# Routing constants in a pool of their own, and a second expert layer with tokens as the stationary side

## The chip, the cores and the metric

The program runs on one core of a Trainium2 chip. The metric is device time in microseconds, lower is better: the median of three runs of the whole program, weights and activations read from the chip's main memory and the result written back to it. Per core there are TensorE (PE, with its weight loads shown apart as PEld), VectorE (DVE), ScalarE (ACT), GpSimd (POOL) and SyncE (SP), which issues most of the transfers.

## The reference

Sliding-window attention over 2304 tokens (4 x 576, 8 heads of 64), then a dense layer pair 512 -> 2048 -> 512 with ELU, then eight experts with 288 tokens each, chosen by a greedy assignment over all sorted logits. Cut to the last part, which the change touches most:

```python
cap = N // E                                   # 2304 // 8 = 288
order = np.argsort(-(x @ w_gate).flatten())
for idx in order:
    tok, e = (int(idx) // E, int(idx) % E)
    if assigned[tok] >= 0 or counts[e] >= cap:
        continue
    assigned[tok] = e
    counts[e] += 1
for e in range(E):
    mask = assigned == e
    h = np.maximum(x[mask] @ w1[e], 0.0)       # (288, 512) @ (512, 1024)
    out[mask] = h @ w2[e]                      # (288, 1024) @ (1024, 512)
```

## The kernel before

**Stages.** Attention goes in 18 chunks of 128 tokens. The first dense layer (`layer1`, L374) goes in six token tiles (256, 256, 256, 512, 512, 512), the second (`layer2`, L470) in 18 chunks; these are woven with attention for as long as it lasts. `gate(t)` (L422) computes the logits of a tile from the hidden values with a precomputed product (L429, L430). Then `routing` (L574) finds the assignment in seven phases on VectorE and POOL, while TensorE works through layer two of the last three tiles (L482) in an order fixed by a table. Last comes the expert stage, one expert after the other.

**Precision.** From the second tile on each factor is a pair of fp16 parts, high and low, and each product is three matmuls: high x high, high x low, low x high.

**First layer of tiles 4 and 5.** For each f, twelve matmuls (L404) fill a PSUM bank `ps_mm` (three of them), ACT reads it into a buffer r (three of them; L407, L408), POOL and DVE make the ELU of it (L413, L414), POOL writes the high half g (L418), DVE the low half (L419). The r buffer is free after L419.

**Routing constants.** `routing_consts(rpool)` (L510) makes some twenty constants on POOL (L520 to L559) in the pool `rpool`, which also holds routing's working tiles. `rpool` and `slabB` (the g of tile 4) are opened when attention's pool is closed, and take its memory.

**The expert stage.** Assigned tokens stand in 24 groups of G = 96, three for each expert. Rows are gathered by an indirect DMA on POOL (L828), transposed (by TensorE for expert 0, L840; by DMA transposes otherwise, L849), and multiplied with W1 (L883: 96 matmuls of 288 columns), with ReLU on ACT (L888) and the low half on DVE (L889). The second layer keeps a 128 x 128 piece of W2 as the stationary side and streams the 288 tokens: 4 output blocks x 8 f x 3 products = 96 matmuls (L917), for the last expert in three thirds of 96 columns, 288 matmuls. Its result is transposed against the order of rows: ACT writes it to OT (L922), TensorE transposes it back in four fp32 transposes per group (L870), ACT evicts again (L872), and POOL scatters the rows (L858).

**The order.** Tile, the scheduler, sorts instructions by priority and a simulated timeline. `weave` interleaves generators by the cost that they yield. In the expert stage ACT and DVE keep program order (`dv`).

Of the kernel before, what the change touches and what calls it, by code (L numbers as in the profile page):

```python
# [7 lines left out]
F32 = mybir.dt.float32  # L8
# [31 lines left out]
def attention_moe_moe2_kernel(ctx: ExitStack, tc: tile.TileContext, q, k, v, w_in, w_out, w_gate, w1, w2, out):  # L40
    nc = tc.nc
# [8 lines left out]
    G = 96  # L50
# [459 lines left out]
    def routing_consts(pool):  # L510
        r = rt
        r["p"] = pool
# [310 lines left out]

    def gather(e):
        for j in range(3):
            XE[e, j] = moe.tile([G, 2 * DM], F16, name="xe", bufs=4)
            a = 3 * e + j
            g = nc.gpsimd.indirect_dma_start(out=XE[e, j], out_offset=None, in_=x2d[:, :],  # L828
                                             in_offset=bass.IndirectOffsetOnAxis(ap=idx[:, a:a + 1], axis=0))
        if e == 0:  # L830
            last["gather"] = g.ins


    def xe_first():
        XET[0] = moe.tile([128, 2, ND, CAP], F16, name="xet")
        for j in range(3):
            px = bank("tp", 2, [128, 2, ND, G], F16)
            for a in range(2):
                for d in range(ND):
                    nc.tensor.transpose(px[:, a, d], XE[0, j][:, (a * ND + d) * 128:(a * ND + d + 1) * 128],  # L840
                                        ident16[:G, :G])
            (nc.scalar.activation(XET[0][:, :, :, j * G:(j + 1) * G], px, AF.Copy) if j % 2 else
             nc.vector.tensor_copy(XET[0][:, :, :, j * G:(j + 1) * G], px))
            yield 400

    def xe_t(e):
        XET[e] = moe.tile([128, 2, ND, CAP], F16, name="xet")
        for j in range(3):
            nc.sync.dma_start_transpose(out=XET[e].rearrange("p a d c -> p (a d) c")[:, :, j * G:(j + 1) * G], in_=XE[e, j])  # L849
            yield 400  # L850
# [4 lines left out]
    def scatter(e, j, orow):  # L855
        a = 3 * e + j
        nc.gpsimd.memset(spacer, 0.0)
        st = nc.gpsimd.indirect_dma_start(out=out, out_offset=bass.IndirectOffsetOnAxis(ap=idx[:, a:a + 1], axis=0),  # L858
                                          in_=orow, in_offset=None)
        for o in scat:  # L860
            tc.declare_no_dep(st.ins, o.ins, reason="other rows")
        scat.append(st)


    def o_rows(e):
        yield 450
        for j in range(3):
            po = bank("pv", 1, [128, ND, 128])
            for d in range(ND):
                nc.tensor.transpose(po[:G, d], OT[e][:, d, j * G:(j + 1) * G], ident)  # L870
            orow = moe.tile([G, DM], F32, name="orow")
            dv(nc.scalar.activation(orow, po[:G], AF.Copy))  # L872
            scatter(e, j, orow)
            yield 450

    def expert(e, xe=None, tail=None):
# [20 lines left out]
        for j in range(3 if first else 0):  # L897
            next(xe, None)
            for f in range(first):
                products(phs[f], f, slice(j * G, j * G + G))  # L900
# [8 lines left out]
        OT[e] = moe.tile([128, ND, CAP], F32, name="oT")  # L909

        for r in [slice(j * G, j * G + G) for j in range(3)] if e == E - 1 else [slice(0, CAP)]:
            n = r.stop - r.start

            def add(po, d, f, m):
                w = W2[e][f // 2]
                for a, b in ((0, 0), (0, 1), (1, 0)):
                    nc.tensor.matmul(po[:, :n], w[:, a, f % 2, d * 128:(d + 1) * 128], H2[e][:, b, f, r],  # L917
                                     start=m == 0, stop=m == 3 * NF2 - 1)
                    m += 1

            def leave(po, d):
                dv(nc.scalar.activation(OT[e][:, d, r], po[:, :n], AF.Copy, scale=2.0 ** -18))  # L922

            if r.start == 0:

                pos = [bank(("sc", "tp")[d % 2], 2) for d in range(ND)]
                for f in range(NF2):
                    for d in range(ND):
                        add(pos[d], d, f, 3 * f)
                    yield 1475 * n / CAP  # L930
                for d in range(ND):
                    leave(pos[d], d)
                continue
            for d in range(ND):
                po = bank(("sc", "tp")[d % 2], 2)
                for f in range(NF2):
                    add(po, d, f, 3 * f)
                leave(po, d)
                yield 2950 * n / CAP
                if tail is not None and d == 0:  # L940
                    next(tail)
# [23 lines left out]
    w64_ctx.close()  # L965
    a2.append(a2_ctx.enter_context(tc.tile_pool(name="a2", bufs=2)))
# [9 lines left out]
    routing_consts(rpool)  # L976
# [37 lines left out]
    for e in range(E):  # L1014
        if e == E - 1:
            tail = o_rows(e)
            next(tail)
        ss = [(expert(e, xe_first() if e == 0 else None, tail if e == E - 1 else None), 24000.0)]
# [4 lines left out]
        if e > 0:  # L1023
            ss.append((o_rows(e - 1), 2000.0))
        weave(*ss)
    weave((tail, 1))
# [30 lines left out]
```

## Time and profile before

| | us |
|---|---|
| median of 3 runs | 792.12 (789.75 to 794.94) |
| profiled execution | 792.14 |
| its span, first to last instruction | 790.1 |
| TensorE busy | 742.5 (94%), mean granted clock 0.97 |
| VectorE busy | 427.7 (54%) |
| ScalarE busy | 374.0 (47%) |
| POOL busy | 184.2 (23%) |

Busy times are unions over the span, and matmuls are pipelined: the step from one matmul's start to the next one's start tells the cost of one in a dense stream, and the duration shown for one matmul is longer than that. The granted clock is 1.00 at 2.4 GHz and 0.50 at 1.2 GHz. The expert stage is the last fourth of the span.

### The profile page before, as it was taken

The numbers are of one execution on the slowest core, as the hardware profiler recorded it, in microseconds if no ns is written. First come the engines' busy times: TensorE is split into PE (matmuls) and PEld (weight loads), VectorE is DVE, ScalarE is ACT, GpSimd is POOL, SyncE is SP. The second block draws the span as 40 slices with busy tenths as digits, with TensorE's granted clock in tenths as the row PEclk, the third lists the DMA queues.
The fourth block names the chain that finished last, engine by engine and source line by source line (L and its number), as shares of the span: only waits on it lengthen the run. The fifth ranks groups of instructions, "written<-read, shape, count | busy, mean of one in ns | idle before, by whom it ended". The sixth has DMA issues, their size and how long they took to land.

```text
span 790.1 us, 16243 instructions
## 1 busy us (share of the span) xinstructions
PE 742.5 (94%) x6610; PEld 479.6 (61%) x6610; DVE 427.7 (54%) x1001; ACT 374.0 (47%) x903; POOL 184.2 (23%) x290
## 2 busy tenths in 40 slices
PE   6886988899999999889999999999989999999996
PEld 4665867655555555534545444444468888888886
DVE  3799499823332665455453555555726555555530
ACT  4467797655634654344455221010025565555632
POOL 3000000000001435344461433434141221211102
PEclk9898999999999999979999999999979999999999
DMA  9995357436455542001000211220058788987401
GB/s 279 319 216 134 62 131 194 114 82 143 96 116 113 94 67 81 3 0 54 2 24 31 81 53 41 73 75 28 15 134 266 193 252 245 261 248 201 170 22 51
DMA packets 137658, 94.06 MB, mean 119 GB/s; under 512 B 116592, under 2 KB 116592, under 8 KB 137584
## 3 DMA queue, kind: packets, MB, share of 16 engines
q1 hardware_dynamic: 134512, 83.59, 39.8%
q0 software_dynamic: 3072, 9.44, 4.6%
q8 instruction: 52, 0.85, 0.5%
q14 instruction: 22, 0.18, 0.1%
HBM read 73.68 MB, written 9.44 MB: 105 GB/s over the span
## 4 chain that ended last, share of the span: by engine, by line
PE 75%; DVE 10%; DMA 5%; ACT 4%; issue 2%; POOL 2%; SPq 1%; POOLq 0%; DVEq 0%
PE ps_mm L482 23%; PE ps_mm L404 17%; PE ps_mm L883 12%; PE ps_sc L917 6%; PE ps_tp L917 6%; DMA slab<-in_moe_w_in_dram 2%; PE ps_pv L312 2%; PE ps_tp L302 2%; DMA wg<-in_moe_w_gate_dram 1%; PE ps_pv L870 1%; PE ps_sc L651 1%; DVE b L106 1%; ACT slab L111 1%; ACT sm L290 1%; DVE r L414 1%
## 5 line engine op out<-in xcount | busy, mean ns | idle before, releaser
L482 PE MATMUL ps_mm<-slab,g 128*128 128x512 f16 x864 | 211.8, 381 | 0.0
L404 PE MATMUL ps_mm<-xt,slab 128*128 128x512 f16 (+1 forms) x960 | 177.8, 343 | 7.8 <-DVE r L414 6.9
L404 PEld LDWEIGHTS <-slab 128*128 128x128 f16 x960 | 93.0, 99 | 79.3 <-issue 12.8
L482 PEld LDWEIGHTS <-g 128*128 128x128 f16 x864 | 74.4, 98 | 71.4 <-issue 2.2
L883 PE MATMUL ps_mm<-xet,slab 128*128 128x288 f16 (+1 forms) x840 | 102.7, 281 | 0.0
L883 PEld LDWEIGHTS <-slab 128*128 128x128 f16 x840 | 78.4, 101 | 17.5
L917 PEld LDWEIGHTS <-slab 128*128 128x128 f16 x960 | 78.6, 98 | 16.2
L818 DVE SCALAR_TENSOR_TENSOR slab<-raw,slab 128x512 f16<-128x512 f32 x112 | 72.9, 688 | 20.3 <-ACT slab L817 17.8
L462 POOL TENSOR_TENSOR xs<-r,xs 128x512 f16<-128x512 f32 x17 | 20.0, 1178 | 261.3 <-ACT xs L494 230.6
L407 ACT ACTIVATE r<-ps_mm 128x512 f32<-128x512 f32 x64 | 38.6, 602 | 72.3 <-PE ps_mm L404 58.6
L917 PE MATMUL ps_sc<-h,slab 128*128 128x288 f16 (+1 forms) x480 | 70.2, 262 | 0.0
L917 PE MATMUL ps_tp<-h,slab 128*128 128x288 f16 (+1 forms) x480 | 69.9, 262 | 0.0
L414 DVE TENSOR_TENSOR r<-ps_mm,r 128x512 f32<-128x512 f32 x64 | 44.0, 688 | 38.6 <-POOL r L413 29.2
L817 ACT ACTIVATE slab<-raw 128x512 f16<-128x512 f32 x112 | 64.5, 620 | 0.0
L889 DVE SCALAR_TENSOR_TENSOR h<-ps_mm,h 128x288 f16<-128x288 f32 x64 | 29.2, 456 | 63.6 <-ACT h L888 58.1
L419 DVE TENSOR_TENSOR g<-r,g 128x512 f16<-128x512 f32 x64 | 45.9, 722 | 32.2 <-POOL g L418 26.4
L493 ACT ACTIVATE r<-ps_mm 128x512 f32<-128x512 f32 x17 | 10.2, 599 | 108.4 <-PE ps_mm L482 108.4
L290 ACT ACTIVATE sm<-ps_sc,mx 128x128 f32<-128x128 f32 x144 | 50.8, 380 | 19.4 <-DVE mx L288 19.0
L888 ACT ACTIVATE h<-ps_mm 128x288 f16<-128x288 f32 x64 | 26.3, 411 | 48.1 <-PE ps_mm L883 47.2
L858 POOL DMA_INDIRECT out_dram<-orow,idx x24 | 22.2, 926 | 114.5 <-ACT orow L872 113.1
L413 POOL TENSOR_SCALAR r<-r 128x512 f32<-128x512 f32 x48 | 38.5, 802 | 41.0 <-ACT r L408 39.9
L408 ACT ACTIVATE r<-r 128x512 f32<-128x512 f32 x64 | 40.7, 638 | 1.5
(209 smaller groups left out, 1047.2 us busy)
## 6 DMA issues: line engine op xcount, KB each, us to landing
raw<-in_moe_w_dram SPq DMA_DIRECT2D x32, 1024.0 KB, 5.4
slab<-in_moe_w_in_dram SPq DMA_DIRECT2D x16, 512.0 KB, 9.7
st<-in_moe_w_out_dram SPq DMA_DIRECT2D x16, 512.0 KB, 5.5
x2d<-xs SPq DMA_DIRECT2D x18, 256.0 KB, 2.0
vp<-in_v_dram SPq DMA_DIRECT2D x34, 128.0 KB, 3.8
qn<-in_q_dram SPq DMA_DIRECT2D x16, 256.0 KB, 3.8
kn<-in_k_dram SPq DMA_DIRECT2D x16, 256.0 KB, 5.0
vn<-in_v_dram SPq DMA_DIRECT2D x16, 256.0 KB, 3.4
```

The lines of the kernel that those rows point to most:

```text
L290: nc.scalar.activation(P[c, blk][:, i], SC[blk][:, i], AF.Exp, bias=mx[:, blk, i:i + 1], accum_out=rs[:, blk, i:i + 1])
L404: nc.tensor.matmul(ph[:, i], wi[d, (f + i) // 8][:, a, (f + i) % 8 * 128:((f + i) % 8 + 1) * 128], XT[t][:, b, d, :n], start=m == 0, stop= ...
L407: nc.scalar.activation(r, ph, AF.Relu, scale=-1.0 / A_H)
L408: last["act"] = nc.scalar.activation(r, r, AF.Exp, scale=-1.0).ins
L413: nc.gpsimd.tensor_scalar(r, r, -1.0, A_H, op0=OP.add, op1=OP.mult)
L414: nc.vector.tensor_tensor(r, ph, r, op=OP.max)
L419: nc.vector.tensor_tensor(lo, r, hi, op=OP.subtract)
L482: pe(nc.tensor.matmul(px, g[:, f % fg, a, 128 * i:128 * i + 128], wo[f // 2][:, b, f % 2, :], start=m == 0, stop=m == 3 * NF - 1))
L817: dv(nc.scalar.activation(t[:, 0, c], st[:, g], AF.Copy, scale=64.0))
L818: dv(nc.vector.scalar_tensor_tensor(t[:, 1, c], st[:, g], 64.0, t[:, 0, c], op0=OP.mult, op1=OP.subtract))
L883: nc.tensor.matmul(ph[:, r], W1[e][d][:, a, f * 128:(f + 1) * 128], XET[e][:, b, d, r], start=m == 0, stop=m == 3 * ND - 1)
L917: nc.tensor.matmul(po[:, :n], w[:, a, f % 2, d * 128:(d + 1) * 128], H2[e][:, b, f, r], start=m == 0, stop=m == 3 * NF2 - 1)
```

## The change

Group size G becomes 128, so that the 2304 assigned tokens stand in 18 chunks. An expert's 288 tokens are 2.25 chunks: `share(c)` tells which experts have rows in chunk c. Twelve chunks belong to one expert, six to two. Gathers and scatters go by chunk (18 of each instead of 24), and what is transposed goes by the parts that a chunk and an expert have in common (`parts_of`), cut where a DMA transpose needs it.

The second expert layer is turned round: the tokens' hidden values H2 are the stationary side and W2 streams with 512 columns, so PSUM holds rows, which ACT evicts once and POOL scatters. OT and the transposes L870 are gone. In a chunk shared by two experts, the stationary side is cut into 64 or 32 tokens, each written to its own partitions of one PSUM bank: chunks 4 and 13 in halves, chunks 2, 6, 11 and 15 in quarters.

The routing constants get a pool `rconsts` of their own and are made ahead of layer two's first chunk.

```diff
-    G = 96
+    G = 128
@@ routing_consts
-        r["p"] = pool
@@ the expert stage
+    def share(c):
+        out = []
+        for e in range(E):
+            lo, hi = max(G * c, CAP * e), min(G * c + G, CAP * e + CAP)
+            if lo < hi:
+                out.append((e, lo - CAP * e, hi - CAP * e, lo - G * c))
+        return out
+
+    def chunks_of(e):
+        return [c for c in range(NG) if any(x[0] == e for x in share(c))]
...
     def gather(e):
...
+        for c in chunks_of(e):
+            if c in XE:
+                continue
+            XE[c] = moe.tile([G, 2 * DM], F16, name="xe", bufs=5)
+            nc.gpsimd.indirect_dma_start(out=XE[c], out_offset=None, in_=x2d[:, :],
+                                         in_offset=bass.IndirectOffsetOnAxis(ap=idx[:, c:c + 1], axis=0))
+
+    def parts_of(e):
+        return [(c, s0, s1, p0) for c in chunks_of(e) for x, s0, s1, p0 in share(c) if x == e]
...
     def xe_first():
...
+        for c, s0, s1, p0 in parts_of(0):
+            n = s1 - s0
...
     def xe_t(e):
...
+        for c, s0, s1, p0 in parts_of(e):
+            while s0 < s1:
+                n = min(s1 - s0, 128 if p0 == 0 else 64 if p0 == 64 else 32)
+                nc.sync.dma_start_transpose(out=XET[e].rearrange("p a d c -> p (a d) c")[:, :, s0:s0 + n],
+                                            in_=XE[c][p0:p0 + n])
+                s0, p0 = s0 + n, p0 + n
             yield 400
...
-    def o_rows(e):
-        yield 450
-        for j in range(3):
-            po = bank("pv", 1, [128, ND, 128])
-            for d in range(ND):
-                nc.tensor.transpose(po[:G, d], OT[e][:, d, j * G:(j + 1) * G], ident)
-            orow = moe.tile([G, DM], F32, name="orow")
-            dv(nc.scalar.activation(orow, po[:G], AF.Copy))
-            scatter(e, j, orow)
-            yield 450
+    def o_rows(c):
+        held = share(c)
+        step = G if len(held) == 1 else 64 if all(x[3] % 64 == 0 for x in held) else 32
+        po = bank(("sc", "tp")[c % 2], 2)
+        m = 0
+        for f in range(NF2):
+            for a, b in ((0, 0), (0, 1), (1, 0)):
+                for e, s0, s1, p0 in held:
+                    for k in range(0, s1 - s0, step):
+                        nc.tensor.matmul(po[p0 + k:p0 + k + step], H2[e][:, a, f, s0 + k:s0 + k + step],
+                                         W2[e][f // 2][:, b, f % 2, :], start=m == 0, stop=m == 3 * NF2 - 1)
+                m += 1
+            yield 650
+        orow = moe.tile([G, DM], F32, name="orow")
+        dv(nc.scalar.activation(orow, po, AF.Copy, scale=2.0 ** -18))
+        scatter(c, orow)
@@ expert
-        for j in range(3 if first else 0):
+        for c, s0, s1, p0 in parts_of(e) if first else ():
             next(xe, None)
             for f in range(first):
-                products(phs[f], f, slice(j * G, j * G + G))
+                products(phs[f], f, slice(s0, s1))
...
+        for c in chunks_of(e):
+            if share(c)[-1][0] == e:
+                yield from o_rows(c)
@@ the main program
     w64_ctx.close()
+    routing_consts(ctx.enter_context(tc.tile_pool(name="rconsts", bufs=1, side="right")))
     a2.append(a2_ctx.enter_context(tc.tile_pool(name="a2", bufs=2)))
...
     rpool = late.enter_context(tc.tile_pool(name="rpool", bufs=2))
-    routing_consts(rpool)
+    rt["p"] = rpool
```

**Where instructions stand.** First POOL, where tile 4's first layer begins (r and g are its hidden values, k the first constants). Before:

```order
L413 TENSOR_SCALAR r<-r 128x512 x3
L520 IOTA k_3859 128x96
L520 IOTA k_3862 128x96
L520 IOTA k_3864 128x96
L530 MEMSET wt 32x128 x4
...
L559 MEMSET done 128x144
L418 TENSOR_SCALAR g<-r 128x512 x3
L534 AFFINE_SELECT third<-third 96x96
```

After:

```order
L413 TENSOR_SCALAR r<-r 128x512 x3
L418 TENSOR_SCALAR g<-r 128x512 x3
L413 TENSOR_SCALAR r<-r 128x512
L418 TENSOR_SCALAR g<-r 128x512
L413 TENSOR_SCALAR r<-r 128x512 x2
```

The constants now stand ahead of POOL's first L462 of layer two, and nothing is left between the L413 and the L418.

Second DVE at the same place, from attention's last L330 on (L432 reads out a chunk of gate(3) from one of two PSUM banks). Before:

```order
L330 SCALAR_TENSOR_TENSOR xt<-ps_pv,xt 128x4x128
L432 TENSOR_REDUCE logits<-ps_tp 128x8 x4
L419 TENSOR_TENSOR g<-r,g 128x512 x3
L414 TENSOR_TENSOR r<-ps_mm,r 128x512 x2
L419 TENSOR_TENSOR g<-r,g 128x512
```

After:

```order
L330 SCALAR_TENSOR_TENSOR xt<-ps_pv,xt 128x4x128
L419 TENSOR_TENSOR g<-r,g 128x512
L432 TENSOR_REDUCE logits<-ps_tp 128x8
L419 TENSOR_TENSOR g<-r,g 128x512
L432 TENSOR_REDUCE logits<-ps_tp 128x8
L419 TENSOR_TENSOR g<-r,g 128x512
L432 TENSOR_REDUCE logits<-ps_tp 128x8 x2
L414 TENSOR_TENSOR r<-ps_mm,r 128x512
```

The L419 have moved ahead of the reductions, and on ACT L408 has moved up behind the first L407.

Third PE in expert 1, where chunk 2 (32 rows of expert 0, h_6904, and 96 of expert 1, h_7243) is computed. Two of its matmuls stand between first-layer matmuls (L903, which is L883 before):

```order
L903 MATMUL ps_mm<-xet,slab 128x288
L888 LDWEIGHTS h_7243
L888 MATMUL ps_sc<-slab,h_7243 32x512
L888 LDWEIGHTS h_6904
L888 MATMUL ps_sc<-slab,h_6904 32x512
L903 LDWEIGHTS slab
L903 MATMUL ps_mm<-xet,slab 128x288
```

Most of the chunk follows the expert's first layer in one piece, three quarters of one expert and one of the other in turn:

```order
L888 LDWEIGHTS h_6904
L888 MATMUL ps_sc<-slab,h_6904 32x512
L888 LDWEIGHTS h_7243
L888 MATMUL ps_sc<-slab,h_7243 32x512
L888 LDWEIGHTS h_7243
L888 MATMUL ps_sc<-slab,h_7243 32x512
L888 LDWEIGHTS h_7243
L888 MATMUL ps_sc<-slab,h_7243 32x512
```

Before, W2's full 128 x 128 pieces (L917) and the transposes (L870) stood at these places.

## Rows read from the trace of the kernel before

**Rows 1.** The page's first part: engine, busy us, share of the span, instructions.
```profile
PE 742.5 (94%) x6610; PEld 479.6 (61%) x6610; DVE 427.7 (54%) x1001; ACT 374.0 (47%) x903; POOL 184.2 (23%) x290
```

**Rows 2.** By stretches: length, busy of PE, PEld, DVE, ACT, POOL; clock, DMA, GB/s.
```profile
332.10:339.08 6.98, 0.99 (x12) 0.66 (x13) 4.40 (x5) 3.19 (x6) 4.22 (x16) 0.60 0.01 2
339.08:343.70 4.62, 4.62 (x11) 1.57 (x11) 3.33 (x5) 0.04 (x1) 3.68 (x5) 0.50 0.00 0
...
600.00:782.60 182.60, 182.60 (x1691) 150.62 (x1688) 91.23 (x159) 100.45 (x220) 34.34 (x37) 1.00 0.70 197
```

**Rows 3.** Timeline of POOL: start, us, instruction, idle before and its releaser.
```profile
177.38 1.16 POOL L462 TENSOR_TENSOR xs<-r,xs 128x512 f16<-128x512 f32 x1 [168.87 <-ACT xs L494]
...
328.88 1.83 POOL L520 IOTA k<- 128x96 f32 x3 [12.17 <-PE ps_pv L312]
...
332.61 0.21 POOL L559 MEMSET done<- 128x144 bf16 x1
332.80 1.77 POOL L418 TENSOR_SCALAR g<-r 128x512 f16<-128x512 f32 x3
...
335.02 0.28 POOL L547 TENSOR_SCALAR_AFFINE_SELECT tri<-tri 128x128 bf16<-128x128 bf16 x1
```

**Rows 4.** Timelines of VectorE, ScalarE and TensorE in the same pause.
```profile
333.44 3.61 DVE L419 TENSOR_TENSOR g<-r,g 128x512 f16<-128x512 f32 x3 [1.24 <-POOL g L418]
...
335.88 1.20 ACT L407 ACTIVATE r<-ps_mm 128x512 f32<-128x512 f32 x2 [6.50 <-DVE g L419]
...
339.08 5.02 PE L404 MATMUL ps_mm<-xt,slab 128*128 128x512 f16 x12 [1.76 <-DVE r L414]
```

**Rows 5.** TensorE's timeline in the expert stage, and one group by line and form.
```profile
603.78 0.53 PE L917 MATMUL ps_sc<-h,slab 128*128 128x288 f16 x3
...
607.08 0.53 PE L917 MATMUL ps_tp<-h,slab 128*128 128x288 f16 x3
...
624.49 0.60 PE L870 MATMUL ps_pv<-ident,oT 128*96 128x128 f32 x4
624.93 0.53 PE L917 MATMUL ps_sc<-h,slab 128*128 128x288 f16 x3
...
781.62 1.18 PE L917 MATMUL ps_tp<-h,slab 128*128 128x96 f16 x24
...
L917 PE MATMUL ps_sc<-h,slab 128*128 128x96 f16 x144 | 9.0, 206 | 0.0
```

**Rows 6.** TensorE's timeline around small tiles, and durations of two lines.
```profile
178.03 0.81 PE L482 MATMUL ps_mm<-slab,g 128*128 128x512 f16 x3
178.77 0.69 PE L312 MATMUL ps_pv<-pt,vn 128*64 128x64 f32 x16
179.39 0.66 PE L248 MATMUL ps_tp<-ident,kn 128*128 128x128 f32 x4
179.97 0.41 PE L263 MATMUL ps_sc<-masks,identb 64*64 64x512 bf16 x4
180.32 0.39 PE L482 MATMUL ps_mm<-slab,g 128*128 128x512 f16 x1
...
L312 PE MATMUL ps_pv<-pt,vn x304: 218/222/369, 16.8 to 328.5; 128*64 128x64 f32 x144, 64*64 64x64 f32 x8
...
557.38 0.23 PE L659 MATMUL ps_sc<-co,third 96*32 96x8 f16 x3
...
L659 PE MATMUL ps_sc<-co,third 96*32 96x8 f16 x105 | 8.1, 171 | 0.0
```

**Rows 7.** Timelines of VectorE, POOL and TensorE between routing and the experts.
```profile
549.84 0.93 POOL L733 TENSOR_SCALAR i<-i 128x864 f16<-128x864 f16 x1
...
570.19 2.02 DVE L773 TENSOR_TENSOR oB<-sa,i 128x864 f16<-128x864 f16 x2
...
575.84 1.17 POOL L828 DMA_INDIRECT xe<-x2d,idx  x1 [12.22 <-DMA x2d<-xs]
...
579.36 0.80 PE L840 MATMUL ps_tp<-ident,xe 96*128 96x96 f16 x8 [3.14 <-DMA xe<-x2d,idx]
```

More of the change, by code (lines that the diff above doesn't have):

```diff
@@ L822, in split_expert @@
                 yield 500
-    def gather(e):
-        for j in range(3):
[L826 to L831, printed above, removed]
+    def share(c):
[7 more added lines that the diff above has]
+        return [c for c in range(NG) if any(x[0] == e for x in share(c))]
+    def gather(e):
+        for c in chunks_of(e):
[6 more added lines that the diff above has]
+        return [(c, s0, s1, p0) for c in chunks_of(e) for x, s0, s1, p0 in share(c) if x == e]
     def xe_first():
         XET[0] = moe.tile([128, 2, ND, CAP], F16, name="xet")
-        for j in range(3):
+        for c, s0, s1, p0 in parts_of(0):
+            n = s1 - s0
             px = bank("tp", 2, [128, 2, ND, G], F16)
@@ L839, in xe_first @@
                 for d in range(ND):
[L840 to L843, printed above, removed]
+                    nc.tensor.transpose(px[:, a, d, :n], XE[c][p0:p0 + n, (a * ND + d) * 128:(a * ND + d + 1) * 128],
+                                        ident16[p0:p0 + n, p0:p0 + n])
+            (nc.scalar.activation(XET[0][:, :, :, s0:s1], px[:, :, :, :n], AF.Copy) if c % 2 else
+             nc.vector.tensor_copy(XET[0][:, :, :, s0:s1], px[:, :, :, :n]))
             yield 400
@@ L847, in xe_t @@
         XET[e] = moe.tile([128, 2, ND, CAP], F16, name="xet")
-        for j in range(3):
-            nc.sync.dma_start_transpose(out=XET[e].rearrange("p a d c -> p (a d) c")[:, :, j * G:(j + 1) * G], in_=XE[e, j])
+        for c, s0, s1, p0 in parts_of(e):
[4 more added lines that the diff above has]
+                s0, p0 = s0 + n, p0 + n
             yield 400
@@ L853, in attention_moe_moe2_kernel, with scatter @@
     spacer = consts.tile([1, 1], F32)
-    def scatter(e, j, orow):
-        a = 3 * e + j
+    def scatter(c, orow):
         nc.gpsimd.memset(spacer, 0.0)
-        st = nc.gpsimd.indirect_dma_start(out=out, out_offset=bass.IndirectOffsetOnAxis(ap=idx[:, a:a + 1], axis=0),
+        st = nc.gpsimd.indirect_dma_start(out=out, out_offset=bass.IndirectOffsetOnAxis(ap=idx[:, c:c + 1], axis=0),
                                           in_=orow, in_offset=None)
@@ L862, in scatter, with expert @@
         scat.append(st)
-    def o_rows(e):
-        yield 450
-        for j in range(3):
-            po = bank("pv", 1, [128, ND, 128])
-            for d in range(ND):
-                nc.tensor.transpose(po[:G, d], OT[e][:, d, j * G:(j + 1) * G], ident)
-            orow = moe.tile([G, DM], F32, name="orow")
-            dv(nc.scalar.activation(orow, po[:G], AF.Copy))
-            scatter(e, j, orow)
-            yield 450
-    def expert(e, xe=None, tail=None):
+    def o_rows(c):
[14 more added lines that the diff above has]
+        scatter(c, orow)
+    def expert(e, xe=None):
         H2[e] = moe.tile([128, 2, NF2, CAP], F16, name="h2")
@@ L908, in expert @@
             yield 1475
[L909 to L941, printed above, removed]
+        for c in chunks_of(e):
+            if share(c)[-1][0] == e:
+                yield from o_rows(c)
     UT = 256 * 192 / 2.4
@@ L1014, in attention_moe_moe2_kernel @@
     for e in range(E):
[L1015 to L1018, printed above, removed]
+        ss = [(expert(e, xe_first() if e == 0 else None), 24000.0)]
         if e + 1 < E:
@@ L1022, in attention_moe_moe2_kernel @@
         ss.append((chain(take(sp, 8 if e < E - 1 else 0), xe_t(e + 1) if e < E - 1 else iter(()), sp), 9400.0))
-        if e > 0:
-            ss.append((o_rows(e - 1), 2000.0))
         weave(*ss)
-    weave((tail, 1))
 _INS = ['q', 'k', 'v', 'moe_w_in', 'moe_w_out', 'moe2_w_gate', 'moe2_w1', 'moe2_w2']
```

## The prediction

> **What bounds the kernel now.** I read the page's busy times first: TensorE is busy for 94% of the span [rows 1], so only idle time of TensorE, slow time of its clock, or matmul work itself is worth anything. The table by stretches then shows where it is not dense. From 600 to 782.6 us, the expert stage, it is busy for 182.60 of 182.60 us at full clock: there the time is the sum of the matmuls. From 332.1 to 339.08, between the gate of tile 3 and the first layer of tile 4, it works 0.99 us out of 6.98, and from 339.08 to 343.7 it is busy all the time at clock 0.50, which is 1.2 GHz [rows 2]. The change touches both places. Its two halves are independent, so I cost them apart.
>
> **A, the constants.** POOL's timeline shows the cause of the pause. The constants stand in POOL's queue ahead of three L418, the high halves of tile 4's first hidden values. The first constant waits 12.17 us for the attention's last L312, since rpool takes attention's memory. Then the constants run from 328.88 to 332.82, and only then come the three L418, with five more constants behind them until 335.30 [rows 3]. VectorE's three L419 need those L418. They begin at 333.44 and last 3.61 us together; the first is over only shortly before ACT starts again at 335.88, half a microsecond after POOL's last constant, so it made little headway beside POOL's work. ACT was waiting for the r buffer which that L419 frees, and PE's L404 follows 3.2 us behind ACT [rows 4]. TensorE queues L404 behind the second gate's first matmuls, which wait for the same L419.
>
> After the change the constants run ahead of layer two. POOL's first work there waits 168.87 us before it begins at 177.38 [rows 3], so some 4.7 us of constants are hidden; if that cover were gone, they would cost at most those 4.7. The first L418 still waits for the attention's memory, until 328.88. Three L418 then end at 330.65. By the measured half microsecond the first L419 ends at 331.2, ACT resumes at 331.25 instead of 335.88 (4.6 us earlier), and since the new order puts L408 directly behind the first L407, one 0.6 us step leaves the chain. Some of that is lost where VectorE now has L419 ahead of the reductions that free the gate's PSUM banks: I take 0.2 off. L404 resumes near 334.1: 5.0 us gained. The clock: eleven L404 ran at 1.2 GHz in 4.62 us [rows 2], so half of that, 2.3 us, was lost to the clock. It fell inside the old pause; the new one is some 2 us with gate matmuls in it, and nothing shows whether it still falls. I take 1.0 of 2.3. A = 6.0 us, with 5.0 and 7.3 as its ends.
>
> **B, the second expert layer.** Before: 672 matmuls of 288 columns. The rows at 603.78 and 607.08 have 27 between them, 0.122 us each: 82.1 us. Expert 7 has 288 of 96 columns. 24 of these take 1.18 us; without the last one's own 0.21 that is 0.042 for each of 23 steps: 12.1 us. 24 groups of four transposes at 0.44 us (from the group's start to the next matmul's) make 10.6 us [rows 5]. Together 104.8.
>
> After: 12 chunks lie inside one expert, each of 24 matmuls of 512 columns. A step of that size is 0.21 to 0.22 us (three L482 in 0.81 us, the last one's 0.39 taken off) [rows 6]; I use 0.216: 62.2 us. Six chunks straddle two experts. Two of these are cut into halves of 64 rows, four into quarters of 32, and each part streams all 512 columns: 480 matmuls. The sum rests on whether the two or four parts run beside each other. No row shows four quarters. Two neighbours do: L263's four 64x64 tiles of 512 columns take 0.41 us together, where one matmul alone has 0.39, and L482 starts only 0.35 after them; L312's 16 instructions on 64-column halves take 0.69 us, of which the last one's own duration is 0.22, so 0.47 us from the first start to the last [rows 6]. Four fp32 transposes of 128 columns take 0.44 [rows 5], so 64 such columns stream for 0.055; fifteen steps in series would be 0.83, not 0.47. Halves run side by side, so I take quarters to do so too, at 0.216 us a round.
>
> From the instruction order I count rounds. The scheduler puts small pieces of a shared chunk between first-layer matmuls; a round that is cut costs as much as a full one. The six chunks need 26, 24, 26, 26, 24 and 25 rounds, 151 in all, 32.6 us. They stand in 29 pieces, and each piece changes the shape of the array twice. Entering costs 0.09 us (L482's third start is 178.46, L312 begins at 178.77, 0.31 instead of 0.216) and leaving 0.10 (last L312 start 179.24, 0.055 of streaming, next start 179.39) [rows 6]: 29 x 0.19 = 5.5 us. After: 62.2 + 32.6 + 5.5 = 100.3. B = 4.5, less 0.2 for staggered starts: 4.3 us. ScalarE also drops its OT evictions, but in this stage it is no limit, so that counts nothing; the loads, splits and gathers are as many bytes as before and TensorE waited for none of them in 182.6 us. The last scatter has 128 rows instead of 96 behind one eviction less: nil, within 0.5 either way.
>
> By the Trainium skill ("TensorE: Matmul & The Clock Gate", Part 3, The mechanism), a weight load overlaps running matmuls only when its row group differs, and column parts all share their rows. By that rule each round would wait for its loads and the result is the third rival's. The rows of L312 speak against it: two loads and two matmuls fit in each 0.06 us (0.47 over 8 pairs) [rows 6], hardly more than the streaming alone.
>
> **C, what it costs.** Larger groups make the last two routing comparisons L773 (2.02 us) a third longer, 0.67, of which I take 0.5 since L766 and L768 shrink by a quarter. VectorE's part of x2d's last rows stands behind them, and the gather waits for that write until 575.84. POOL's L733 (0.93 us) grows by 0.3 beside VectorE's routing chain. The first gather carries 128 rows, and PE's first transpose at 579.36 waits for it [rows 7]: 0.4. Expert 0's first transposes and products come in parts of 128, 128 and 32 at the low clock: 0.6. C = 1.8, between 0.8 and 3.
>
> **Sum.** 6.0 + 4.3 - 1.8 = 8.5 us off the profiled execution's 792.14 (span 790.1 and 2 around it), which is the median, 792.12. Predicted: 783.6, own range 780 to 787.
>
> **The rivals.** First, the pause at 332 stays: the release of attention's memory still holds the L418, and if VectorE or PE's order holds L404 to nearly its old time, A falls to 1 and the time is 788.6. For it: the L418 wait for the same release. Against: four of the seven microseconds are plainly constants. Second, C is larger, the gathers above all, at twice the cost or more: 786 to 788. Third, the quarters' weight loads stand in front of their streams. Three L659 of 32 columns, load and matmul, take 0.23 us, the last one's own 0.17 among them, so a step of 0.03 [rows 6]. Four steps per round are 0.12, and 151 rounds make 18 us: 801.7, slower than before. It decides from 0.056 us a round (8.5 over 151). Fourth, parts do not run together at all: 480 x 0.216 = 103.7 instead of 32.6, 71 us more, 854.5; the L312 rows all but exclude it.
>
> **How the numbers follow.** Main case 0.70; pause stays 0.10; larger C 0.09; loads in front 0.08; no overlap 0.03. One per cent, about what a measurement here can tell, is 784.2 below and 800.0 above. Of the main case about two thirds lie below 784.2, which with its upside gives faster 0.46; same 0.43, from the rest of it and the next two; slower 0.11 from the last two. The range 779.5 to 790.5 holds the main case and most of the next two.
>
> **What the profile would show.** A right: L418 starting within 0.2 us of attention's last L312, L404 back by 334.5. B right: 32-row matmuls starting four at a time every 0.216 us, no L870, the stage from expert 0's first product to the end some 4 us shorter. Wrong if rounds are 0.27 us or longer, if TensorE idles between experts, or if L404 comes back after 337.

## The result, and the profile after

The change makes the kernel faster: 782.86 us median of 11 runs (781.48 to 788.34) against 792.56 for the kernel before in the same comparison, a ratio of 0.989 with a 95% interval of 0.987 to 0.991. The prediction was 783.6, in a range of 779.5 to 790.5. The profiled execution took 781.48 us (span 779.6), against 792.14 (span 790.1).

The first part of the page after, with the same columns as [rows 1]:

```profile
PE 736.7 (94%) x6322; PEld 430.1 (55%) x6322; DVE 427.0 (55%) x1001; ACT 358.9 (46%) x857; POOL 176.2 (23%) x272
```

TensorE has 5.8 us less to do and waits some 4.7 us less. POOL's timeline shows where the constants went, and that the three L418 now come right behind attention, beside [rows 3]:

```profile
155.88 1.83 POOL L519 IOTA k<- 128x96 f32 x3 [148.27 <-DVE slab L112]
...
160.27 0.28 POOL L546 TENSOR_SCALAR_AFFINE_SELECT tri<-tri 128x128 bf16<-128x128 bf16 x1
178.12 1.16 POOL L462 TENSOR_TENSOR xs<-r,xs 128x512 f16<-128x512 f32 x1 [17.57 <-ACT xs L494]
...
329.64 2.28 POOL L418 TENSOR_SCALAR g<-r 128x512 f16<-128x512 f32 x3 [12.19 <-PE ps_pv L312]
```

The constants run from 155.9 to 160.6, and POOL still has 17.57 us to spare before its first L462. VectorE, ScalarE and TensorE behind the L418, beside [rows 4]:

```profile
330.77 0.68 DVE L419 TENSOR_TENSOR g<-r,g 128x512 f16<-128x512 f32 x1
...
331.48 0.60 ACT L407 ACTIVATE r<-ps_mm 128x512 f32<-128x512 f32 x1 [1.36 <-DVE g L419]
...
334.46 4.60 PE L404 MATMUL ps_mm<-xt,slab 128*128 128x512 f16 x12 [0.29 <-DVE r L414]
```

L404 is back at 334.46 instead of 339.08, although this execution was 0.75 us later at attention's end (the last group of L312 began at 328.80, before at 328.05). What is left of the pause, and of the low clock behind it, beside [rows 2]:

```profile
331.40:334.46 3.06, 2.45 (x77) 2.26 (x76) 2.60 (x8) 2.95 (x6) 1.32 (x2) 0.50 0.03 8
334.46:338.23 3.77, 3.77 (x9) 1.28 (x9) 2.54 (x4) 0.35 (x1) 3.39 (x5) 0.50 0.00 0
```

TensorE idles for 0.6 us of these 6.8, but the clock is at 0.50 throughout; before, the low stretch lasted until 343.7.

For the expert stage I take the stretch from the end of expert 0's first three groups of products to TensorE's last matmul, in which both kernels have the same first-layer work. Before and after:

```profile
588.34:783.46 195.12, 195.11 (x1792) 160.33 (x1788) 100.64 (x176) 108.70 (x238) 36.12 (x39) 1.00 0.69 195
```

```profile
582.00:773.37 191.37, 191.37 (x1504) 112.78 (x1500) 101.06 (x176) 93.43 (x192) 28.87 (x28) 1.00 0.66 198
```

Both are busy from end to end at full clock, so the difference, 3.75 us, is the difference of the two second layers. In after, TensorE's timeline of chunk 2 shows the quarters. The scheduler cuts a chunk into pieces between first-layer matmuls (L903), and not always at a full round, hence counts that are no multiples of four; two earlier pieces, of 1 and 7 quarters, complete the 96:

```profile
606.77 0.40 PE L888 MATMUL ps_sc<-slab,h 128*32 128x512 f16 x3
607.10 3.12 PE L903 MATMUL ps_mm<-xet,slab 128*128 128x288 f16 x24
610.14 0.39 PE L888 MATMUL ps_sc<-slab,h 128*32 128x512 f16 x2
610.47 1.65 PE L903 MATMUL ps_mm<-xet,slab 128*128 128x288 f16 x12
612.04 0.39 PE L888 MATMUL ps_sc<-slab,h 128*32 128x512 f16 x2
612.37 1.64 PE L903 MATMUL ps_mm<-xet,slab 128*128 128x288 f16 x12
613.94 4.71 PE L888 MATMUL ps_sc<-slab,h 128*32 128x512 f16 x81
618.58 1.68 PE L888 MATMUL ps_tp<-slab,h 128*128 128x512 f16 x7
```

From 613.94 to 618.58 there are 21 rounds in 4.64 us, 0.216 each with 0.10 for the way out: a round of four quarters costs what one whole matmul does. One cut round stands from 612.04 to 612.37, 0.33 instead of 0.216; and from 610.47 to 612.04 twelve L903 take 1.57, of which 12 x 0.1225 (the step from one start to the next) = 1.47 are their own. So a piece costs 0.10 us on the way in and 0.11 on the way out.

Between routing and the experts, beside [rows 7]:

```profile
543.50 1.17 POOL L732 TENSOR_SCALAR i<-i 128x1152 f16<-128x1152 f16 x1
...
563.99 2.62 DVE L772 TENSOR_TENSOR oB<-sa,i 128x1152 f16<-128x1152 f16 x2
...
570.23 1.19 POOL L839 DMA_INDIRECT xe<-x2d,idx  x1 [12.70 <-DMA x2d<-xs]
...
573.85 1.01 PE L852 MATMUL ps_tp<-ident,xe 128*128 128x128 f16 x8 [3.33 <-DMA xe<-x2d,idx]
```

L732 and L772 are longer by the third that their tiles grew (0.24 and 0.60 us); from the gather's issue to the first transpose it is 3.62 us, against 3.52 before.

### The profile page after: what moved, and what is told of

It is laid out like the page before. It is cut to its first block, busy times and chain, and to the rows that moved or that the text cites. A ratio compares the mean times of both kernels' runs of the same rounds, so it can differ in the third digit from the quotient of the medians.

```text
span 779.6 us, 15588 instructions
## 1 busy us (share of the span) xinstructions
PE 736.7 (94%) x6322; PEld 430.1 (55%) x6322; DVE 427.0 (55%) x1001; ACT 358.9 (46%) x857; POOL 176.2 (23%) x272
## 4 chain that ended last, share of the span: by engine, by line
PE 65%; issue 14%; DVE 11%; ACT 5%; DMA 3%; POOL 2%; SPq 1%; POOLq 0%; DVEq 0%
PE ps_mm L482 23%; PE ps_mm L404 17%; PE ps_mm L903 6%; PE ps_sc L888 3%; PE ps_tp L888 2%; PE ps_pv L312 2%; PE ps_tp L302 2%; PE ps_mm L392 2%; ACT sm L290 1%; POOL out_dram L873 1%; PE ps_sc L650 1%; DVE b L106 1%; ACT slab L111 1%; DVE r L414 1%; DVE slab L106 1%
## 5 line engine op out<-in xcount | busy, mean ns | idle before, releaser
L404 PE MATMUL ps_mm<-xt,slab 128*128 128x512 f16 (+1 forms) x960 | 178.0, 343 | 6.1 <-DVE r L414 5.2
L404 PEld LDWEIGHTS <-slab 128*128 128x128 f16 x960 | 93.3, 100 | 77.7 <-issue 10.9
L903 PE MATMUL ps_mm<-xet,slab 128*128 128x288 f16 (+2 forms) x840 | 101.6, 277 | 0.0
L903 PEld LDWEIGHTS <-slab 128*128 128x128 f16 x840 | 75.2, 98 | 25.2 <-issue 6.0
L888 PEld LDWEIGHTS <-h 128*32 128x32 f16 (+2 forms) x768 | 43.1, 98 | 53.0 <-issue 9.8
L407 ACT ACTIVATE r<-ps_mm 128x512 f32<-128x512 f32 x64 | 38.5, 602 | 66.5 <-PE ps_mm L404 59.1
L414 DVE TENSOR_TENSOR r<-ps_mm,r 128x512 f32<-128x512 f32 x64 | 44.0, 688 | 36.3 <-POOL r L413 26.8
L419 DVE TENSOR_TENSOR g<-r,g 128x512 f16<-128x512 f32 x64 | 44.6, 700 | 31.8 <-POOL g L418 25.9
L888 PE MATMUL ps_sc<-slab,h 128*32 128x512 f16 (+2 forms) x384 | 53.4, 381 | 0.0
L888 PE MATMUL ps_tp<-slab,h 128*32 128x512 f16 (+2 forms) x384 | 53.0, 380 | 0.0
L413 POOL TENSOR_SCALAR r<-r 128x512 f32<-128x512 f32 x48 | 38.5, 802 | 38.5 <-ACT r L408 37.7
L462 POOL TENSOR_TENSOR xs<-r,xs 128x512 f16<-128x512 f32 x17 | 20.0, 1177 | 110.0 <-ACT xs L494 79.3
L418 POOL TENSOR_SCALAR g<-r 128x512 f16<-128x512 f32 x48 | 31.4, 655 | 47.0 <-DVE r L414 28.2
L408 ACT ACTIVATE r<-r 128x512 f32<-128x512 f32 x64 | 40.7, 638 | 1.5
## 6 DMA issues: line engine op xcount, KB each, us to landing
slab<-in_moe_w_in_dram SPq DMA_DIRECT2D x16, 512.0 KB, 10.5
```

The costliest lines, as they stand in the source:

```text
L404: nc.tensor.matmul(ph[:, i], wi[d, (f + i) // 8][:, a, (f + i) % 8 * 128:((f + i) % 8 + 1) * 128], XT[t][:, b, d, :n], start=m == 0, stop= ...
L407: nc.scalar.activation(r, ph, AF.Relu, scale=-1.0 / A_H)
L408: last["act"] = nc.scalar.activation(r, r, AF.Exp, scale=-1.0).ins
L413: nc.gpsimd.tensor_scalar(r, r, -1.0, A_H, op0=OP.add, op1=OP.mult)
L414: nc.vector.tensor_tensor(r, ph, r, op=OP.max)
L419: nc.vector.tensor_tensor(lo, r, hi, op=OP.subtract)
```

## The experiments

The theory: the two halves of the change are independent. A, the constants' place in POOL's queue, gives 5 to 6 us; B, the turned second layer, gives some 4, since a round of parts costs as much as one whole matmul and only the changes of shape cost extra; C, the larger groups, takes 2 back. C has no run of its own; it is read from the traces. The rivals are those of the prediction, and one more: that chance in TensorE's clock, which differs from execution to execution, made the difference. All runs of one comparison share the runs of the kernel before (medians 791.4 to 792.6).

**Each half alone.** a_alone has only the constants' new place:

```diff
 in before:
-        r["p"] = pool
...
     w64_ctx.close()
+    routing_consts(ctx.enter_context(tc.tile_pool(name="rconsts", bufs=1, side="right")))
...
-    routing_consts(rpool)
+    rt["p"] = rpool
```

> The kernel before with one edit: the constants go to a pool of their own and are made ahead of layer two; group size and second expert layer stay. Theory (the constants in POOL's queue were the pause): L404 is back within 6 us of attention's last L312 instead of 11, the last L482 ends some 6 us earlier than before, the expert stage is as long as before: 786.5 us (785.0 to 788.5). Rival 1 (the release of attention's memory or VectorE's order holds L404 and the changed kernel got its gain from elsewhere): 790 or more. Rival 2 (the gain is chance in the clock at the start of the program): 792.

Measured: 786.88 us, ratio 0.9927 (0.9901 to 0.9952). b_alone is the changed kernel with that one edit undone:

```diff
 in after:
-    routing_consts(ctx.enter_context(tc.tile_pool(name="rconsts", bufs=1, side="right")))
...
     rt["p"] = rpool
+    routing_consts(rpool)
```

> The changed kernel with one edit undone: the constants stand in rpool again, behind attention; G = 128 and the turned second layer stay. Theory (the two halves are independent): what is left of 9.7 us after 6.1 for the constants, so 3.6 faster than before: 789.0 us (787.0 to 790.5), with the pause of 7 us at 332 as before. Rival (the expert stage alone brings nearly all of it): 785 or less. Rival (the larger groups cost what the second layer gives): 792 or more.

Measured: 789.16 us, ratio 0.9964 (0.9943 to 0.9986). TensorE's L404 behind the pause and the expert stage (from expert 0's first products, as above) in a_alone:

```profile
333.33 4.56 PE L404 MATMUL ps_mm<-xt,slab 128*128 128x512 f16 x12 [0.30 <-DVE r L414]
```

```profile
579.65:774.78 195.13, 195.12 (x1792) 160.35 (x1789) 100.30 (x176) 108.34 (x238) 38.15 (x40) 1.00 0.69 197
```

and in b_alone:

```profile
341.05 2.29 PE L404 MATMUL ps_mm<-xt,slab 128*128 128x512 f16 x5 [1.70 <-DVE r L414]
```

```profile
589.69:781.07 191.38, 191.38 (x1504) 112.82 (x1500) 101.13 (x176) 93.61 (x192) 29.30 (x28) 1.00 0.65 198
```

The expert stage repeats to 0.01 us: 195.12 and 195.13 with the old second layer, 191.37 and 191.38 with the new one. L404 comes back 5.20 us after the start of attention's last matmul in a_alone and in after, 9.68 in b_alone and 10.56 before. By the medians A is 5.3 us and B less C is 3.0, together 8.4 (8.6 by the ratios), inside the interval of the whole (7.4 to 10.3 us). The halves add up, and no rival of the two expectations holds.

**The constants a little later.** Two things could have made the old pause: that the L418 stood behind the constants, and that POOL's work beside it held up VectorE's L419 (the first of the three in [rows 4] took 2.41 us by itself, the line below the edit). consts_late keeps the constants behind attention but calls for them after tile 5's first layer, so that the scheduler puts them behind the three L418:

```diff
 in before:
-        r["p"] = pool
...
-    routing_consts(rpool)
+    rt["p"] = rpool
...
+    routing_consts(rpool)
     pinned.append(1)
```

The first L419 of the pause in the kernel before:

```profile
333.44 2.41 DVE L419 TENSOR_TENSOR g<-r,g 128x512 f16<-128x512 f32 x1 [1.24 <-POOL g L418]
```

> The kernel before with the constants moved only a little: still behind attention in rpool, but in POOL's queue after the first three L418 instead of ahead of them. Theory (two things made the pause: the place in POOL's queue, and VectorE's L419 being slow beside POOL's constants): L418 starts at attention's end as in a_alone, but the first L419 takes some 2 us instead of 0.68 and L413 stands behind the constants, so L404 is back some 2 to 3 us earlier than before: 789.5 us (788 to 791). Rival (the place in the queue alone): as a_alone, 786.9. Rival (POOL's work beside VectorE alone, or the constants' length wherever they stand): 792.

Measured: 790.08 us, ratio 0.9978 (0.9962 to 0.9994). POOL, VectorE and TensorE in consts_late:

```profile
328.74 2.28 POOL L418 TENSOR_SCALAR g<-r 128x512 f16<-128x512 f32 x3 [12.19 <-PE ps_pv L312]
330.99 1.82 POOL L519 IOTA k<- 128x96 f32 x3
...
334.99 0.62 POOL L413 TENSOR_SCALAR r<-r 128x512 f32<-128x512 f32 x1
```

```profile
329.87 0.68 DVE L419 TENSOR_TENSOR g<-r,g 128x512 f16<-128x512 f32 x1
...
331.57 0.67 DVE L419 TENSOR_TENSOR g<-r,g 128x512 f16<-128x512 f32 x1
...
335.64 0.69 DVE L414 TENSOR_TENSOR r<-ps_mm,r 128x512 f32<-128x512 f32 x1 [2.79 <-POOL r L413]
...
338.58 2.70 DVE L419 TENSOR_TENSOR g<-r,g 128x512 f16<-128x512 f32 x3
```

```profile
336.39 5.95 PE L404 MATMUL ps_mm<-xt,slab 128*128 128x512 f16 x18 [3.19 <-DVE r L414]
```

The time is as the theory said, the way there only in part. The first three L419 are not slowed: 0.68 beside L418, 1.01 for the next, and 0.67 beside the first constants (L519), as in a_alone, without constants there (0.68, 1.01, 0.68). The loss against a_alone is the queue: L413, the next step of the ELU, waits behind the constants until 334.99 (331.69 in a_alone), L414 behind L413, and L404 comes back 8.03 us after attention's last matmul began, 2.8 later than in a_alone. So a constant costs the time for which the next needed POOL instruction stands behind it, and moving it behind one such instruction only hands the wait to the next. L419 can still be slow beside POOL: the next three here take 2.70 us, from 338.58 on, beside three L418 (from 337.93). And the last five constants have no L419 beside them here; in b_alone they do, as in the kernel before, and two of them take 0.71 and 0.62 us (0.27 and 0.20 here). So this run does not clear those five. Why the first L419 took as much as 2.41 us in the kernel before is not settled: in b_alone, with the same POOL instructions in the same order, the three of them took 2.77 us instead of 3.61.

**What holds the rest of the pause.** After the change the L418 still wait 12.19 us for attention's memory. g_free gives tile 4's first two g buffers from slabA, where two are free at that point:

```diff
 in after:
-    l4, l5 = layer1(4, [slabB] * 8), layer1(5, [slabB] * 2 + [slabA] * 6)
+    l4, l5 = layer1(4, [slabA] * 2 + [slabB] * 6), layer1(5, [slabB] * 4 + [slabA] * 4)
```

> The changed kernel with tile 4's first two g buffers from slabA, where two are free, instead of slabB, which waits for attention's memory (tile 5 takes two more from slabB in exchange). Theory (what is left of the pause after the change is L418's wait for that memory): L418 starts some 10 us earlier, TensorE has no idle time between 327 and 339; 0.9 us of idle go, and with them up to 3.1 us that L404 and the gate's small matmuls lose at 1.2 GHz: 779.0 us if the clock stays up, 782.0 if it falls all the same because of the gate's small matmuls. Rival (the free buffers are not free, the wait moves to slabA): 783 or more, with a new wait on L418 or on tile 5's first layer.

Measured: 780.32 us, ratio 0.9827 (0.9797 to 0.9857), 2.5 us below the changed kernel. By stretches (length, busy time of PE, PEld, DVE, ACT, POOL, then clock, DMA, GB/s) in g_free:

```profile
326.00:330.00 4.00, 4.00 (x25) 2.32 (x23) 2.36 (x4) 2.61 (x6) 1.75 (x2) 1.00 0.00 0
330.00:334.00 4.00, 4.00 (x101) 3.20 (x100) 1.47 (x4) 2.25 (x4) 1.72 (x3) 1.00 0.02 4
334.00:338.00 4.00, 4.00 (x35) 1.99 (x32) 3.13 (x7) 0.92 (x2) 1.31 (x3) 1.00 0.01 2
```

TensorE has no idle time and its clock stays at 1.00, where in after it fell to 0.50 from 331.4 to 338.2. The release of attention's memory was the rest of the pause, and the low clock went with it. The profiled execution itself gained only 0.4 us on after's (781.07 against 781.48): it ran at 0.50 from 411.3 to 414.7, where after's did not, and 3.5 us longer before attention's end.

**The pieces.** one_piece holds TensorE to program order in the expert stage, so that the six shared chunks are six pieces:

```diff
 in after, the matmuls of o_rows and of products:
-                        nc.tensor.matmul(po[p0 + k:p0 + k + step], ...)
+                        dv(nc.tensor.matmul(po[p0 + k:p0 + k + step], ...))
...
-                    nc.tensor.matmul(ph[:, r], ...)
+                    dv(nc.tensor.matmul(ph[:, r], ...))
```

> The changed kernel with TensorE held to program order in the expert stage, so that each of the six shared chunks is one piece instead of 29 pieces between first-layer matmuls. Theory (each piece costs two changes of the array's shape, 0.094 us in and 0.125 out by the trace of after): 23 pieces x 0.22 = 5.0 us less, 777.9 us (776.5 to 779.5), TensorE without idle time in the stage. Rival 1 (the pieces fill time in which first-layer matmuls would wait for a PSUM bank): TensorE idles ahead of L903 by as much, 782 or more. Rival 2 (a change of shape is free and the 0.22 are the rounds themselves): 782.9.

Measured: 777.54 us, ratio 0.9803 (0.9779 to 0.9827). The stage and a shared chunk in one_piece:

```profile
584.85:769.50 184.65, 184.56 (x1500) 114.31 (x1499) 100.74 (x175) 93.17 (x191) 29.18 (x28) 1.00 0.67 203
```

```profile
602.81 11.92 PE L903 MATMUL ps_mm<-xet,slab 128*128 128x288 f16 x96
614.66 5.36 PE L888 MATMUL ps_sc<-slab,h 128*32 128x512 f16 x96
619.96 5.35 PE L888 MATMUL ps_tp<-slab,h 128*128 128x512 f16 x24
625.15 5.06 PE L903 MATMUL ps_mm<-xet,slab 128*128 128x288 f16 x40
```

The stage is 6.7 us shorter than in after: 24 pieces fewer at 0.21 are 5.0, and 8 rounds fewer (cut rounds no longer cost a full one) at 0.216 are 1.7. TensorE idles for 0.09 us, so the pieces had filled no wait that was there. The 24 rounds of quarters take 5.30 with the way out, 24 whole matmuls 5.19. Rival 2, that a change of shape is free, would have given nothing. Between the medians 5.3 of the 6.7 us show; the profiled execution of one_piece had a mean granted clock of 0.967, after's 0.973.

**More loads in a round.** all_quarters cuts the twelve whole chunks into quarters too:

```diff
 in after, o_rows:
-        step = G if len(held) == 1 else 64 if all(x[3] % 64 == 0 for x in held) else 32
+        step = 32
```

> The changed kernel with every chunk of the second expert layer cut into quarters of 32 tokens, the twelve whole ones too: 288 rounds go from one load and one matmul to four of each. Theory (the quarters' loads and streams run beside each other): a round stays at 0.216 us; only the number of pieces between first-layer matmuls goes from 29 to 36, 7 x 0.21 = 1.5 us more: 784.4 us (782.5 to 787). Rival (each quarter's load stands in front of its stream, 0.03 us each): 0.12 x 288 = 35 us more, 818. Rival (they overlap in part): 0.03 us a round would already be 8.6 us, 791.5.

Measured: 787.8 us, ratio 0.9947 (0.9928 to 0.9965): 4.9 us more than the changed kernel, against 1.5 foreseen, and far from 818. To see whether the quarters or the cuts cost it, all_quarters_one makes the same edit in one_piece.

> one_piece with every chunk cut into quarters: all_quarters without its cut rounds, since nothing stands between the quarters of a chunk. It tells where the 4.9 us of all_quarters came from, of which 1.5 were foreseen. Theory (cut pieces and cut rounds: 37 pieces and 447 rounds there, against 30 and 440 in the changed kernel; here 8 pieces and 432 rounds, against 6 and 432 in one_piece): 777.54 + 2 x 0.2 = 777.9 us (776.5 to 779.5). Rival (a round of four quarters is a little longer than a whole one, 0.0135 us by the 3.9 us of TensorE's time over 288 rounds): 781.4.

Measured: 779.32 us, ratio 0.9837 (0.9807 to 0.9867), 1.8 us more than one_piece. The whole stage in all_quarters, then the two places in all_quarters_one where three chunks stand in a row:

```profile
584.63:779.91 195.28, 194.96 (x2463) 115.49 (x2460) 100.72 (x176) 93.30 (x192) 27.75 (x28) 1.00 0.64 193
```

```profile
660.72 5.36 PE L888 MATMUL ps_sc<-slab,h 128*32 128x512 f16 x96
665.91 5.35 PE L888 MATMUL ps_tp<-slab,h 128*32 128x512 f16 x96
671.09 3.06 PE L888 MATMUL ps_sc<-slab,h 128*32 128x512 f16 x52
674.44 3.09 PE L888 MATMUL ps_sc<-slab,h 128*32 128x512 f16 x44 [0.29 <-issue]
677.46 2.75 PE L903 MATMUL ps_mm<-xet,slab 128*128 128x288 f16 x21
...
761.54 5.35 PE L888 MATMUL ps_sc<-slab,h 128*32 128x512 f16 x96
766.72 5.35 PE L888 MATMUL ps_tp<-slab,h 128*32 128x512 f16 x96
```

The first two chunks take 5.19 and 5.18 us, as 24 whole matmuls do: four loads and four matmuls fit in a round without a cost. The third is uneven, 6.37 with a stop put down to issue. That is not the length of the row: in the other row, at the end of the stage, the third chunk is as long as the second (5.35 to the end of its last matmul). The stage of all_quarters_one is 1.8 us longer than one_piece's: the two pieces more are 0.4, the uneven chunk 1.2. In all_quarters the stage is 3.9 us longer than in after: 7 pieces more are 1.5, and by counting the instruction order 447 rounds instead of 440 are 1.5 more. That leaves 0.9. The same chunk is uneven there too, 6.52 us (674.06 to 680.58) instead of 5.29, so the count comes out 0.3 too high. The expectation had left out the cut rounds and did not know of the uneven chunk.

**The parts of a chunk one after the other.** expert_by_expert moves the loop over experts outside the loop over f, so that one expert's part is finished before the other's begins:

```diff
 in after, o_rows:
-        for f in range(NF2):
-            for a, b in ((0, 0), (0, 1), (1, 0)):
-                for e, s0, s1, p0 in held:
+        for e, s0, s1, p0 in held:
+            m = 0
+            for f in range(NF2):
+                for a, b in ((0, 0), (0, 1), (1, 0)):
...
```

> The changed kernel with the two experts' parts of each shared chunk one after the other, instead of side by side in one round: the same 480 matmuls, but 288 rounds for the six chunks instead of 144 (without counting cut ones). Theory (a round costs 0.216 us whether one, two, three or four parts are in it): 144 x 0.216 = 31 us more, 814 us (808 to 820). Rival (the cost is by matmuls or loads, not by rounds): 783 to 786, as the number of either is the same.

Measured: 807.4 us, ratio 1.0205 (1.0167 to 1.0243): 24.5 more than the changed kernel, just below the expected 808 to 820. The stage, and the last piece of chunk 2 with what follows it:

```profile
585.49:800.84 215.35, 215.35 (x1504) 123.83 (x1500) 101.26 (x176) 93.42 (x192) 28.32 (x28) 1.00 0.56 175
```

```profile
619.56 6.24 PE L889 MATMUL ps_sc<-slab,h 128*32 128x512 f16 x80
625.74 5.35 PE L889 MATMUL ps_tp<-slab,h 128*128 128x512 f16 x24
```

The cost goes by rounds, not by matmuls or loads, which are as many as in after: the stage is 24.0 us longer. By the order of the instructions there are 286 rounds instead of 152, which is 28.9 us, less 1.0 for five pieces fewer, so 27.9. The piece shows where the missing 3.9 are. In program order it holds 8 quarters of the first expert, then 72 of the second in threes, 31 rounds; it takes 6.18 us until the next chunk starts, 28 rounds and the way out. Its first 0.9 us, and the 0.2 us behind them, in narrow windows of the same timeline (a row counts what runs in its window, what began earlier too):

```profile
619.56 1.04 PE L889 MATMUL ps_sc<-slab,h 128*32 128x512 f16 x4
...
620.22 0.62 PE L889 MATMUL ps_sc<-slab,h 128*32 128x512 f16 x5
```

Four quarters start one by one, 0.216 us apart; then, besides the one of 620.22, four are new at once: the first three of the second expert start beside the fifth of the first, while three of the first expert's are still to come. The profile does not show the columns, but no other reading makes 28 rounds of these 80: some matmuls for idle columns started ahead of earlier ones for busy columns. By their starts the long pieces of the six chunks have 28, 34, 41, 34, 34 and 42 rounds, where program order gives 31, 37, 44, 37, 37 and 45. Three rounds saved in each of six chunks are 18 x 0.216 = 3.9 us.

**Both improvements.** best is one_piece and g_free together, with the edits shown for each.

> The changed kernel with both one_piece (TensorE in program order in the expert stage) and g_free (tile 4's first two g buffers from slabA). Theory (they lie in different stages and add up): 782.9 - 5.4 - 2.5 = 775.0 us (773.5 to 776.5). Rival (one takes the other's gain, through the clock): 777 or more.

Measured: 773.56 us (769.9 to 775.11), ratio 0.9767 (0.9739 to 0.9796), 9.3 us below the changed kernel and 18 below the one before. Its expert stage is one_piece's:

```profile
581.55:766.21 184.66, 184.56 (x1500) 114.35 (x1499) 100.41 (x175) 92.90 (x191) 28.15 (x28) 1.00 0.68 204
```

## Why the prediction was right, point by point

**A, 6.0 us predicted.** The two signs that it named came: L418 started 0.15 us after the end of attention's last L312, and L404 was back at 334.46, even with the later start. From attention's last matmul on, L404 returned 5.36 us sooner, against 5.0. The cover held: 17.57 us of POOL's idle time were left over. Of the 2.3 us that L404 lost to the clock, 1.0 was to come back. In after nine L404 run at 0.50 for 3.77 us, half of which, 1.9, is lost, so 0.4 came back there; the thirteenth L404 starts 5.7 us sooner in all, and a_alone's median gives 5.3. The term was a little high, by the clock. The two causes that it read from [rows 3] and [rows 4] were both in the old pause, but of unequal size. ACT resumed 2.00 us after the end of attention's last L312, instead of 7.14. Of these 5.1 us, 3.9 are L418's earlier start and 1.7 the first L419's shorter time (0.68 instead of 2.41); 0.5 goes the other way, as L330 now stands between the two. Whether L418 or the five constants behind it held up L419 is open: in consts_late those five have no L419 beside them, and the three constants that have one leave it at 0.67.

**B, 4.3 us predicted.** Measured 3.75 between the same two points, and a tail behind the last matmul of 6.25 us instead of 6.62, so 4.1. The sum before was 104.8; what is left of 195.12 without 732 first-layer steps of 0.1225 is 105.4. After, 100.3 against 191.37 less the same 89.7, 101.7. The whole chunks and the rounds came as computed, 0.216. The pieces were a little cheap: 0.21 us each instead of 0.19, and 30 of them with 152 rounds, since one quarter of chunk 2 stands alone at 582.97. The remark that the tail is nil within 0.5 held (0.37 gained).

**Quarters side by side** was the step on which the sign hung. It held, and three runs bear on it: in after 0.216 us a round, in all_quarters_one 24 rounds of four in 5.19 us, and in expert_by_expert 24 us more as soon as the parts stand one behind the other. The rule in the Trainium skill ("TensorE: Matmul & The Clock Gate", Part 3, The mechanism), by which a load overlaps running matmuls only when its row group differs, does not agree with these runs as it stands, though the same section's words on a load into a background weight buffer leave room for them: all four quarters use the same rows, and their loads cost nothing that shows.

**C, 1.8 us predicted.** Between the end of layer two and expert 0's first product there are 12.01 us instead of 10.84: 1.17, of which 0.5 are L772 (predicted 0.5), 0.1 the gather (0.4) and 0.6 the first transposes, which wait for two gathers. L732 lengthened TensorE's wait at routing's first L650 of that phase from 0.79 to 1.15 us, 0.36 (0.3); it is 0.9 in a_alone, with the old size, and 1.2 in b_alone. Expert 0's products until the common point take 5.88 us at a mean clock of 0.91, against 7.30 at 0.66; at full clock that is 5.35 against 4.8, 0.5 more. So the transposes and products cost 1.1 where 0.6 was put, and the gather less than its 0.4. Together 2.0.

**The sum.** 5.3 to 5.7 for A, 4.1 for B and 2.0 for C make 7.4 to 7.8 us, against 8.5 predicted and 9.7 between the medians (7.4 to 10.3 by the interval). In the profiled pair, 10.5 us of span apart, the rest is for the most part in the clock, which gave more in some executions than in others. Expert 0's products ran 5.0 us at 0.50 in the profile before and 1.05 us in the one after, which is 2.0 us that the change did not make. Another 1.4 lie between the pause and the end of layer two, where the one before has 3.4 us at 0.50 from 418.8 on and the one after none, and 0.7 were lost ahead of attention's end. For the medians no trace shows it. That the forecast came within 0.7 us of the median, although its terms came to 0.7 to 1.1 us less than it had put, is in part that luck.

**The rivals.** The pause did not stay, C was not larger by 2 us or more, and neither loads in front (801.7) nor parts in series (854.5) came. expert_by_expert has the parts of two experts in series, though not the quarters of one, and costs 24.

## What to carry to other kernels

An instruction that nobody waits for still costs its whole length where it stands ahead of one that somebody does; look at what is next in its queue, and move it to where the engine has spare time, not just one place back. Small matmuls that write to different columns of the array are priced in rounds, so group them so that every round is full, keep the rounds of a piece together, and count each change of shape (0.2 us here, in and out). When a pause goes away, look at what the next instruction waits for: here a buffer in memory that something else still held cost another 2.5 us, some 0.9 of it idle time and the rest, by estimate, the low clock behind it.

## What the runs showed of the hardware that was not expected

- A matmul can start ahead of an earlier one in program order when that one's columns are busy and its own are idle: in expert_by_expert three rounds in each of six chunks, 3.9 us. The Trainium skill ("TensorE: Matmul & The Clock Gate", Part 3, The mechanism) says that matmuls start and end in program order; this trace does not agree, by the starts from 619.56 on and by the rounds saved.
- A row of quarters does not always stay at 0.216 us a round. One chunk, the third in its row, took 6.37 us instead of 5.18 in all_quarters_one, with a stop of 0.29 put down to issue, and 6.52 in all_quarters. The other row of three stayed even. The DMA engines were busy for 0.94 of the uneven chunk's stretch (671.09 to 677.53) and for 0.14 of the third chunk's in the even row; what TensorE lacked stays open.
- Where the expert stage is the same, its length repeats to 0.01 us from one profile to the next (195.12 and 195.13, 191.37 and 191.38, 184.65 and 184.66), and still single executions of after differ by up to 7 us. In the 11 of them the mean granted clock goes from 0.959 (786.5 us of span) to 0.976 (780.1 and 780.9): a difference of 2 us between single executions says nothing of a change, which is better read in the stretch that it touches.
